# Moving the last pair's transposes of u from SyncE's DMA queue to ScalarE's, and its stores the other way

## The chip, the cores and the metric

The kernel runs on one core of a Trainium2 chip. The metric is the device time of one execution in microseconds. The core has five engines that run side by side and wait for each other through semaphores: TensorE (PE in the profile, with its weight loads apart as PEld), VectorE (DVE), ScalarE (ACT), GpSimd (POOL) and SyncE (SP). DMAs are issued by an engine's instruction stream, in its order: an issue that waits for its data also holds back the issues behind it. SPq and ACTq in the profile are the issues of SyncE and ScalarE.

## The reference

A chunked attention (chunks of 64 rows, 8 batches, 8 heads, 576 rows, head size 64) is followed by a mixing layer on rows of 512 numbers:

```python
attn = softmax(q_c @ k_c.T / sqrt(D)); x = attn @ v_c       # x: (8, 576, 512)
theta = x @ w_theta
zr, zi = x * cos(theta), x * sin(theta)
u = x + einsum('ts,bsd->btd', w_tok_r, zr) + einsum('ts,bsd->btd', w_tok_i, zi)
out = u + maximum(u @ w_ch, 0)
```

The change lies in the last line: u @ w_ch needs u turned (its rows as columns), and out has to be stored.

## The kernel before

The 8 batches are taken as 4 pairs, p = 0 to 3. The 2 x 576 rows of a pair make 9 tiles of 128 rows, j = 0 to 8; tile 4 (MID) holds the last 64 rows of both batches. Nothing is scheduled automatically: the string ORDER (lines 18 to 66) names every step, and each engine gets its share in that order. A step is a kind, a pair and tile, and for products a PSUM slot: `W.34.1` is the product u @ w_ch of pair 3, tile 4, in slot 1.

The steps at the end of a tile are these:

- `Y` (`y`, L480): nine products into ps_y (eighteen of half width for tile 4), the sum over rows of both einsums.
- `y` (`add_x`, L488): VectorE adds x and writes u in float16; there are seven buffers.
- `Ud` (`u_dma`, L505): one DMA transpose turns u (128 x 512) into uT; there are five buffers. The early tiles do this with TensorE instead (`U`, L497) and a copy.
- `W` (`w`, L517): four products of uT with w_ch into ps_uw.
- `w` (`relu_add`, L526): VectorE makes o = max(ps_uw, 0) + u in float32; there are four buffers.
- `st` and `sa` (`store`, L543): the 128 rows of o are two runs of 64 rows in the output, so a tile is stored by two DMAs of 128 KB, the lower half r = 0 and the upper half r = 1. In pairs 0 to 2 `st` stores both halves from SyncE. In pair 3 `st` stores the half r = 0 from SyncE, and `sa` the half r = 1 from ScalarE.

In the text below, "upper" is the half that `sa` stores (r = 1) and "lower" the half that `st` stores in pair 3 (r = 0).

In pair 3 all nine tiles are turned by DMA. The end of ORDER runs, in TensorE's view: Y.36, Y.34, W.35, W.33, W.37, W.36, W.34, and then ten products of zeros (`D`, L157) whose results nobody reads. The order of SyncE's issues in the same stretch: st.38, st.32, st.31, st.30, Ud.37, Ud.33, Ud.36, Ud.34, st.35, st.33, st.37, st.36, st.34. ScalarE issues sa.31, sa.38, sa.32, sa.30, sa.35, sa.33, sa.37, sa.36, sa.34. ScalarE's last computing step is the sine of pair 3, group D; behind it its stream has only these stores.

Each DMA of SyncE and ScalarE reports to one of eight semaphores, taken in turn, and waits for the one that used it before. A buffer of o or uT is written again only when its readers have ended.

Of the kernel before, what the change touches and what calls it, by code (L numbers as in the profile page):

```python
# [69 lines left out]
def kernel(  # L70
# [11 lines left out]
    nc = tc.nc  # L82
# [4 lines left out]
    NDB = DM // P  # L87
    NE = H // 2
    NP = B // 2
# [58 lines left out]
    st = {p: {} for p in range(NP)}  # L148
# [353 lines left out]
    def u_dma(p, j):  # L502
        uT = tmp.tile([P, DM], FP16, name="uT", bufs=5)
        st[p]["uT", j] = uT
        nc.sync.dma_start_transpose(uT.rearrange("p (a c) -> p a c", a=NDB), st[p]["u", j])  # L505

    def u_copy(p, j, copy):
        uT = tmp.tile([P, DM], FP16, name="uT", bufs=5)
# [14 lines left out]
    def relu_add(p, j):  # L523
# [3 lines left out]
            out=o, in0=st[p].pop(("ps_uw", j)), scalar=0.0, in1=u, op0=ALU.max, op1=ALU.add  # L527
        )
        st[p]["o", j] = o

    def store(p, j, queues):
        if j == MID:
            to = [out[2 * p + b, KT * P : S, :] for b in range(2)]
        else:
            bb = int(j > MID)
            jl = j - bb * (MID + 1)
            s0 = (jl // 2) * GT + (jl % 2) * CH
            to = [out[2 * p + bb, s0 + r * P : s0 + r * P + CH, :] for r in range(2)]  # L540
        for r, queue in enumerate(queues):
            if queue is not None:
                queue.dma_start(to[r], st[p]["o", j][half[r]])  # L543
# [45 lines left out]
        "y": add_x,  # L589
        "U": u_t,  # L590
        "Ud": u_dma,
        "ua": lambda p, j: u_copy(p, j, nc.scalar.copy),
        "uv": lambda p, j: u_copy(p, j, nc.vector.tensor_copy),
        "W": w,
        "w": relu_add,
        "st": lambda p, j: store(p, j, (nc.sync, nc.sync if p < 3 else None)),
        "sa": lambda p, j: store(p, j, (None, nc.scalar)),
    }
    with tc.manual_schedule():
        for step in ORDER:  # L600
# [33 lines left out]
```

The softmax here doesn't subtract the row's maximum and nothing guards it: scores larger than these inputs give would overflow.

## Time and profile before

The time is 203.63 us, the median of 3 runs (202.67 to 203.73). The profiled execution has a span of 201.2 us, at the full TensorE clock.

| engine or queue | busy | instructions |
|---|---|---|
| TensorE | 190.9 us (95%) | 2766 |
| VectorE | 127.8 us (63%) | 235 |
| ScalarE | 93.1 us (46%) | 100 |
| GpSimd | 106.3 us (53%) | 133 |
| stores from SyncE | 63 issues of 128 KB | landing after 2.9 us (median) |
| stores from ScalarE | 9 issues of 128 KB | landing after 2.7 us (median) |
| transposes uT<-u from SyncE | 22 issues | landing after 2.5 us (median) |

A busy share says little here, since the end of the kernel differs from its middle. In the last 10 us the engines work in a chain: TensorE makes ps_uw, VectorE o, and a queue stores it. What matters there is which step of that chain ends last for each tile, and what stands ahead of it in its queue. A line of the timeline names the start and the length in us, the engine, the line of the kernel and the tiles (out<-in); in square brackets is the engine's idle time before it and what ended that. Rows marked "x4" are four instructions in a row, and their length is that from the first's start to the last's end, waits between them included.

### The profile page before, as it was taken

What the parts mean: (1) busy time and instruction counts of PE and PEld (TensorE: products, weight loads), DVE (VectorE), ACT (ScalarE), POOL (GpSimd) and SP (SyncE); (2) the same over time, 40 slices, a digit from 0 to 9 for tenths busy, and PEclk for the clock granted to TensorE, in tenths of its full rate; (3) what the DMA queues carried; (4) which work ended last, traced back from release to release, by engine and by line L of the source; (5) the groups of instructions that cost most, each with busy time, mean ns of one, the idle gap of its engine ahead of it and who ended that gap; (6) DMA issues with size and microseconds to landing.
All of it is one profiled execution on the core that took longest, in us unless ns stands there. A gap on an engine that the chain in (4) does not pass through costs nothing.

```text
span 201.2 us, 6347 instructions
## 1 busy us (share of the span) xinstructions
PE 190.9 (95%) x2766; PEld 95.1 (47%) x2766; DVE 127.8 (63%) x235; ACT 93.1 (46%) x100; POOL 106.3 (53%) x133
## 2 busy tenths in 40 slices
PE   7988788999989999999999999999999799899986
PEld 2435455555544645455465555453444344344432
DVE  0015689387886867848874785977584566744461
ACT  2304967456922488797257976427800444000000
POOL 7999999798998999978998800000000000000000
DMA  5999999999999999999999992287777886573775
GB/s 190 173 169 155 159 186 166 153 173 145 168 187 187 155 171 205 181 216 158 161 207 157 153 223 64 45 142 108 159 122 145 174 169 148 121 159 62 214 163 171
DMA packets 140091, 32.01 MB, mean 159 GB/s; under 512 B 132769, under 2 KB 134945, under 8 KB 140065
## 3 DMA queue, kind: packets, MB, share of 16 engines
q0 software_dynamic: 114288, 16.02, 118.9%
q1 hardware_dynamic: 25056, 14.43, 31.2%
q10 hardware_dynamic: 720, 1.18, 2.0%
q8 instruction: 21, 0.34, 0.7%
q14 instruction: 6, 0.04, 0.1%
HBM read 33.06 MB, written 9.44 MB: 211 GB/s over the span
## 4 chain that ended last, share of the span: by engine, by line
PE 56%; DMA 22%; POOL 18%; issue 3%; DVE 0%; SPq 0%; POOLq 0%
PE ps_y L480 24%; PE ps_uw L517 12%; POOL qk L174 11%; PE ps_theta L410 10%; DMA v<-in_v_dram 7%; DMA uT<-u 6%; POOL v L182 4%; DMA qk<-in_q_dram 4%; DMA qk<-in_k_dram 3%; PE ps_qkT L262 2%; PE ps_x L341 2%; PE ps_sT L308 2%; DMA xT<-x 2%; POOL wnat L192 1%; PE ps_idle L157 1%
## 5 line engine op out<-in xcount | busy, mean ns | idle before, releaser
L480 PEld LDWEIGHTS <-wT 128*128 128x128 f16 (+1 forms) x360 | 30.8, 100 | 35.1 <-issue 1.4
L480 PE MATMUL ps_y<-zr,wT 128*128 128x512 f16 (+1 forms) x180 | 44.4, 381 | 0.0
L480 PE MATMUL ps_y<-zi,wT 128*128 128x512 f16 (+1 forms) x180 | 41.8, 379 | 0.0
L488 DVE TENSOR_TENSOR u<-ps_y,x 128x512 f16<-128x512 f32 x36 | 24.8, 688 | 25.0 <-PE ps_y L480 23.5
L517 PE MATMUL ps_uw<-wch,uT 128*128 128x512 f16 x144 | 36.4, 380 | 2.2 <-DMA uT<-u 2.2
L174 POOL DMA_DIRECT2D qk<-in_q_dram x40 | 34.1, 872 | 3.2 <-issue 1.0
L182 POOL DMA_DIRECT2D v<-in_v_dram x40 | 34.0, 869 | 2.9 <-issue 0.9
L174 POOL DMA_DIRECT2D qk<-in_k_dram x40 | 34.1, 869 | 2.3 <-issue 0.9
L410 PE MATMUL ps_theta<-wtheta,xT 128*128 128x512 f16 x144 | 34.3, 380 | 0.6 <-DMA xT<-x 0.5
L426 ACT ACTIVATE cos<-ps_theta,pihalf 128x1024 f16<-128x1024 f32 (+1 forms) x22 | 21.1, 961 | 26.2 <-PE ps_theta L410 23.2
L321 ACT ACTIVATE eT<-ps_sT 128x1024 f16<-128x1024 f32 (+1 forms) x20 | 18.6, 939 | 28.4 <-PE ps_sT L308 28.3
L526 DVE SCALAR_TENSOR_TENSOR o<-ps_uw,u 128x512 f32<-128x512 f32 x36 | 24.7, 689 | 10.9 <-PE ps_uw L517 10.6
L354 DVE TENSOR_TENSOR x<-ps_x,recip 128x512 f16<-128x512 f32 (+1 forms) x40 | 25.5, 638 | 1.4
L517 PEld LDWEIGHTS <-uT 128*128 128x128 f16 x144 | 12.8, 98 | 18.8 <-DMA uT<-u 4.8
L410 PEld LDWEIGHTS <-xT 128*128 128x128 f16 x144 | 13.2, 98 | 16.6 <-DMA xT<-x 0.9
L430 ACT ACTIVATE sin<-ps_theta 128x1024 f16<-128x1024 f32 (+1 forms) x22 | 19.0, 865 | 0.0
L157 PE MATMUL ps_idle<-blank 128*128 128x512 f16 x60 | 17.3, 435 | 1.3 <-DVE pihalf L145 1.2
L287 DVE COPY qkT<-ps_qkT 128x2048 f16<-128x2048 f16 x11 | 13.4, 1218 | 4.0 <-PE ps_qkT L262 4.0
L353 DVE RECIPROCAL recip<-ps_x 128x8 f32<-128x8 f32 (+1 forms) x40 | 7.9, 197 | 11.1 <-PE ps_x L341 10.9
L341 PE MATMUL ps_x<-v,eT 64*64 64x65 f16 x576 | 11.9, 196 | 2.2 <-DMA v<-in_v_dram 1.6
L262 PE MATMUL ps_qkT<-id,qk 64*128 64x64 f16 x576 | 12.0, 191 | 1.0 <-DMA qk<-in_k_dram 0.9
L341 PEld LDWEIGHTS <-eT 64*64 64x64 f16 x576 | 8.3, 106 | 9.4 <-issue 4.8
(42 smaller groups left out, 138.5 us busy)
## 6 DMA issues: line engine op xcount, KB each, us to landing
out_dram<-o SPq DMA_DIRECT2D x63, 128.0 KB, 2.9
qk<-in_q_dram POOLq DMA_DIRECT2D x32, 128.0 KB, 6.5
qk<-in_k_dram POOLq DMA_DIRECT2D x32, 128.0 KB, 6.4
v<-in_v_dram POOLq DMA_DIRECT2D x32, 128.0 KB, 6.5
out_dram<-o ACTq DMA_DIRECT2D x9, 128.0 KB, 2.7
theta<-in_moe_w_theta_dram SPq DMA_DIRECT2D x1, 1024.0 KB, 5.6
wnat<-in_moe_w_tok_r_dram POOLq DMA_DIRECT2D x2, 288.0 KB, 6.0
wnat<-in_moe_w_tok_i_dram POOLq DMA_DIRECT2D x2, 288.0 KB, 6.3
```

The costliest lines, as they stand in the source:

```text
L157: nc.tensor.matmul(ps, blank[:, 0:P], blank, start=True, stop=True)
L174: nc.gpsimd.dma_start(nats[p, g][rows, which, r], (q, k)[which][b, :, t0 : t0 + n, :].rearrange("h s d -> s h d"),)
L182: nc.gpsimd.dma_start(v16[rows, slot + r, :, 0:D], v[b, :, t0 : t0 + n, :].rearrange("h s d -> s h d"),)
L341: nc.tensor.matmul(psv[half[r], to, h4, :], eT[rows, h % 2, r if n == 2 else 0, h // 2, :], v16[rows, slot + (r if n == 2 else 0), h, 0 : ...
L354: nc.vector.tensor_tensor(out=st[p]["x"][:, j0 : j0 + n, f * NE * D : (f + 1) * NE * D].rearrange("p c (h d) -> p c h d", h=NE), in0=psv[: ...
L410: nc.tensor.matmul(ps[:, j * DM : j * DM + DM], xT[:, (j + (t or 0)) * NDB + db, :], wtheta16[:, db, :], start=(db == 0), stop=(db == NDB ...
L426: nc.scalar.activation(out=cos[:, 0:n].rearrange("p a e -> p (a e)"), in_=pin, func=AF.Sin, bias=pihalf, scale=1.0,)
L430: nc.scalar.activation(out=sin[:, 0:n].rearrange("p a e -> p (a e)"), in_=pin, func=AF.Sin)
L480: nc.tensor.matmul(ps[rows], wT[:, kt, cols], z[:, jz, :], start=(kt == 0), stop=(kt == 2 * KT),)
L488: nc.vector.tensor_tensor(out=u, in0=st[p].pop(("ps_y", j))[:, 0:DM], in1=st[p]["x"][:, j], op=ALU.add)
L517: nc.tensor.matmul(ps, uT[:, db * P : db * P + P], wch16[:, db, :], start=(db == 0), stop=(db == NDB - 1),)
L526: nc.vector.scalar_tensor_tensor(out=o, in0=st[p].pop(("ps_uw", j)), scalar=0.0, in1=u, op0=ALU.max, op1=ALU.add)
```

## The change

The nine transposes of pair 3 are issued from ScalarE, and the nine stores of `sa` from SyncE, so that in pair 3 both halves of every tile leave from SyncE's queue. ORDER stays as it is. The purpose is that a transpose does not stand behind stores which wait for o: ScalarE's stream holds only transposes then.

```diff
     def u_dma(p, j):
         uT = tmp.tile([P, DM], FP16, name="uT", bufs=5)
         st[p]["uT", j] = uT
-        nc.sync.dma_start_transpose(uT.rearrange("p (a c) -> p a c", a=NDB), st[p]["u", j])
+        queue = nc.scalar if p == NP - 1 else nc.sync
+        queue.dma_start_transpose(uT.rearrange("p (a c) -> p a c", a=NDB), st[p]["u", j])
...
         "st": lambda p, j: store(p, j, (nc.sync, nc.sync if p < 3 else None)),
-        "sa": lambda p, j: store(p, j, (None, nc.scalar)),
+        "sa": lambda p, j: store(p, j, (None, nc.sync)),
```

SyncE's stream at the end then reads: st.38, sa.38, st.32, st.31, sa.32, sa.30, st.30, sa.35, sa.33, st.35, st.33, and both halves of 37, 36 and 34. ScalarE's: Ud.31, Ud.32, Ud.38, Ud.30, Ud.35, Ud.37, Ud.33, Ud.36, Ud.34.

## The prediction

> **What bounds the kernel now.** I read the chain of waits first, for its last pieces, then the same stretch engine by engine, and last the queues. Only the last pair of batches (p = 3) is touched, so only the time after about 172 us matters. The chain there is TensorE work with three short gaps. Below: start and length in us, and what held the chain.
>
> ```profile
> 171.82 1.04 PE ps_uw L517 x4
> ...
> 189.80 2.44 DMA uT<-u
> 192.24 0.18 DVE o L526
> 192.42 3.18 DMA uT<-u
> 195.65 1.04 PE ps_uw L517 x4
> ```
>
> TensorE itself, in the timeline (in brackets its idle time, and what ended it):
>
> ```profile
> 191.15 1.04 PE L517 MATMUL ps_uw<-wch,uT 128*128 128x512 f16 x4
> 192.35 2.84 PE L517 MATMUL ps_uw<-wch,uT 128*128 128x512 f16 x12 [0.17 <-DMA uT<-u]
> 195.65 1.04 PE L517 MATMUL ps_uw<-wch,uT 128*128 128x512 f16 x4 [0.45 <-DMA uT<-u]
> ```
>
> These are W.35, then W.33, W.37 and W.36, then W.34. The table by stretch has TensorE busy 13.70 of 13.70 us from 177.5 to 191.2, so earlier u transposes of p = 3 held nobody up; only the last five products wait. SyncE's queue shows why:
>
> ```profile
> 185.08 3.27 SPq L543 DMA_DIRECT2D out_dram<-o x4
> 188.45 5.19 SPq L505 DMA_TRANSPOSE uT<-u x4
> 193.74 4.17 SPq L543 DMA_DIRECT2D out_dram<-o x5
> ```
>
> The four transposes of tiles 37, 33, 36 and 34 go out one behind the other, after stores that themselves wait for o. u of tile 37 was ready at 181.3, and its transpose left at 188.45. After the last o (DVE, 196.72 to 197.41) the two stores of tile 34 leave at the same moment from two queues, and this ends the kernel. For these two:
>
> ```profile
> L543 SPq DMA_DIRECT2D out_dram<-o x1: 466/466/466, 197.4 to 197.4; - x1
> L543 ACTq DMA_DIRECT2D out_dram<-o x1: 498/498/498, 197.4 to 197.4; - x1
> ...
> DMA to landing us min/median/max: 2.4/2.5/2.7
> ```
>
> So from the last issue (197.44) to the end of the span (201.25) it is 3.8 us: up to 2.7 to land, some 1.1 to close the program.
>
> **What the skill says.** The Trainium skill, "DMA: Bandwidth & Descriptors", section "Issuing engines are not separate DMA queues": issuing from several engines saves only the issuing sequencer's time, usually small beside the transfer. The trace agrees on the size (0.5 to 0.6 us of issue against 2.4 to land), but here some ten issues stand in a row at the end, so that this saving is what counts. Same page, "Silent corruption: two transposing streams in flight at once": the first transpose of a second issuing engine must wait until those of the first have landed. The built program carries this wait on ScalarE's first transpose (Ud.31); the trace before has one stream only and can't show its cost. Same page, "Anatomy of one DMA": about 2 us per DMA are fixed; its fit for GpSimd's queue gives 2.0 + 131072/436000 = 2.3 us for a store, and the trace has 2.4 to 2.7 for stores from SyncE and ScalarE.
>
> **Transposes to ScalarE: what is won.** ScalarE has nothing after its last sine (167.64, 1.02 us), so each transpose leaves when its u is ready or, if that is later, 1.25 us after the one before it. With u ready as now (end of each add on DVE): Ud.31 waits for Ud.20, issued at 171.86 and 2.42 us on its way, to 174.28; with about four more semaphore waits of some 0.06 us it leaves at 174.5 and lands at about 176.95, where W.31 wants it at 177.53. Ud.32 lands at 178.2 (W.32 at 182.35), Ud.38, 30 and 35 before 185.8, Ud.37 at about 187.0, Ud.33 (u at 186.99) at 189.5, Ud.36 (u at 189.88) at 192.4, Ud.34 (u at 191.95) at 194.45. W.33 can now follow W.35 at 192.03 rather than 192.35, W.36 ends near 194.65, and W.34 starts there instead of 195.65. TensorE ends 1.0 us earlier: 0.17 + 0.45 us of idle time, and twice the 0.18 us by which four products last longer (1.04) than their pitch (0.86) when the pipeline is empty. This is all that the transposes can give, for before 191.2 TensorE is full.
>
> **Stores to SyncE: what is lost.** Until 189.4 SyncE keeps up: tiles 31, 38, 32 and 30 are stored there in pieces while DVE makes the next o. From w.35 on, ten stores stand in SyncE's queue, in the order 35 upper, 33 upper, 35 lower, 33 lower, then 37, 36 and 34 in pairs. Before, they lay five on each queue. The price of one comes from a stretch where nothing waited for data:
>
> ```profile
> 158.01 2.46 SPq L543 DMA_DIRECT2D out_dram<-o x4
> 160.52 1.35 SPq L393 DMA_TRANSPOSE xT<-x  x1
> ```
>
> Four stores and the gaps are 160.52 - 158.01 = 2.51 us, and a wait of its own for o before the first adds some 0.06 a pair: 0.63 to 0.65 us a store. The two ends: 0.47 us (a store that had just waited, as in the two lines above) and 0.82 us (3.27/4, which includes a wait for o). I take 0.63, since most of these find their o ready.
>
> w.35 ends at 192.91 as now. W.33 from 192.03 gives w.33 from 193.10 (1.07 us later, as w.35 follows W.35) to 193.79, so 33 upper leaves at 193.83. Eight stores are behind it; the last starts at 193.83 + 8 x 0.63 = 198.87. VectorE is no longer the limit: o of 37 and 36 are ready at about 194.7 and 195.5, while SyncE reaches them at 195.7 and 197.0. There is one new wait: o of tile 34 takes the buffer of tile 35 (four o buffers), whose lower half now leaves at 194.36 and lands at 196.8. So w.34 runs 196.8 to 197.5 and not from 195.75; but SyncE gets to its stores at 198.25, and this is hidden.
>
> **Sum.** The last store leaves at 198.87 instead of 197.44: + 1.43 us. It lands alone, some 2.4 us later, not as one of two halves issued together of which the slower took 2.7: - 0.3 us. The closing is the same. + 1.1 to + 1.15 us on the span; on the median 203.63 this gives 204.8 us.
>
> **Rivals.** *The store pitch is shorter and the gain pays for most of it.* At 0.55 us a store, the last starts at 193.83 + 4.4 = 198.23, + 0.8 - 0.3 = + 0.5 us: 204.1 us, no change that can be told. For it: the first store after a wait takes 0.47. Against: every unhindered row of stores in the trace has about 0.63.
>
> *ScalarE's transposes become a wait of TensorE.* Ud.31 has only 0.6 us to spare before W.31, and one transpose in this trace (issued 167.15) took 4.6 us to land. If Ud.31 does the same, it lands at 179.1, TensorE stands still for 1.6 us, and everything behind shifts: 203.63 + 1.6 + 1.1 = 206.3 us. For it: the full drain of the other stream. Against: the three transposes after the slow one landed in 2.4 us each.
>
> *Faster: SyncE keeps up.* Then the end is set by w.34. If only TensorE's end counted, w.34 would end at 196.43 and the two stores leave one after the other, the second at 196.95: - 0.5 - 0.3 = - 0.8 us, 202.8 us. For it: TensorE is the bound of the whole kernel, and 1.0 us of its waits does go. Against: with four o buffers w.34 must wait for the lower half of tile 35 to land, and even at 0.47 us a store this is 194.3 + 2.4, so that w.34 ends at 197.4, as now. It takes an issue of about 0.35 us, which no row shows, or luck in an earlier wait, such as that slow transpose which costs TensorE 0.54 us at 171.3.
>
> **How the numbers follow.** Main forecast (+ 0.8 to + 1.6 us) 0.64; shorter pitch 0.22; TensorE waits 0.07; faster 0.07. The line at + 0.5% is 1.02 us, close to the middle of the main case; I put 0.50 of its 0.64 above it, since creeping landings (a row of four lands 2.3, 2.4, 2.4, 2.5 us after issue) and a w.33 that is not earlier (+ 0.3) both lengthen it. Slower: 0.50 + 0.07 = 0.57; same: 0.14 + 0.22 - 0.02 = 0.34; faster: 0.09, with 0.02 from the shorter pitch for the 0.5 us by which runs of the kernel before differ (202.67 to 203.73). The range, from the short pitch at 204.1 less that scatter to the long end of the main case (+ 1.6 and the same scatter), is 203.5 to 205.8.
>
> **What would show it.** Right: no gap of TensorE between W.35 and W.34, W.34 at about 194.7; ten stores back to back on SyncE to about 199.4, the last starting 1.4 us later than now; an idle VectorE before the last o that ends with a store's landing; Ud.31 leaving when Ud.20 has landed. Wrong: SyncE idle between the last stores, a store pitch of 0.5 or 0.8 us, TensorE waiting before W.31, or transposes on ScalarE that take longer than 1.25 us to issue or 2.4 to land.

## The result, and the profile after

The changed kernel takes 204.69 us (median of 20 runs) beside 203.60 us for the kernel before (20 runs): + 1.09 us. The ratio is 1.0067, with a 95% interval of 1.0041 to 1.0093; the forecast was + 1.1 to + 1.15 us and 204.8 us. Here and below the medians are of all runs, and the ratios with their intervals of those within 1.5% of the fastest run of the same kernel, so a ratio need not be the quotient of two medians.

The profiled execution after has a span of 202.9 us, 1.7 us longer than the one before. Of that, 0.7 us was there before the end part begins: w.35, the first of the last five steps on VectorE, ends at 193.61 instead of 192.91. That point lies between 191.8 and 194.2 in the fourteen profiles of this study, and two profiles of one and the same kernel (the one with the late halves and Ud.20 moved, below) have it at 192.68 and 191.82. So I count from it; whether a part of the 0.7 us comes from the change is not shown. From the end of w.35 to the end of the span it was 8.33 us before and is 9.31 after: + 0.98 us.

TensorE after, from W.35 to W.34 in the timeline:

```profile
191.84 4.65 PE L518 MATMUL ps_uw<-wch,uT 128*128 128x512 f16 x20
196.33 1.24 PE L157 MATMUL ps_idle<-blank 128*128 128x512 f16 x3
198.25 1.89 PE L157 MATMUL ps_idle<-blank 128*128 128x512 f16 x8 [0.68 <-DVE o L527]
```

The five products are now one row of twenty matmuls in 4.65 us. Before, they took from 191.15 to 196.69, 5.54 us, in three pieces with a wait for uT between them. The transposes have given 0.89 us. The new gap of 0.68 us stands behind the last product, among the products of zeros.

ScalarE's queue (its last sine, then nothing but transposes) and SyncE's:

```profile
168.48 1.02 ACT L430 ACTIVATE sin<-ps_theta 128x1024 f16<-128x1024 f32 x1
175.53 18.35 ACTq L506 DMA_TRANSPOSE uT<-u  x9
```

```profile
185.77 14.33 SPq L543 DMA_DIRECT2D out_dram<-o  x17
```

SyncE's last store ends its issue at 200.1, where both queues were done at 197.9 before. The ten stores behind w.35, by the tile o:

```profile
L543 SPq DMA_DIRECT2D out_dram<-o x10: 467/568/604, 193.6 to 199.5; - x10
...
DMA to landing us min/median/max: 2.2/2.4/2.4
```

The first row gives the shortest, median and longest issue in ns and when the first and last began. From the end of w.35 to the start of the last issue it is 5.9 us. Before, it was 4.5 us, to a pair that left together from two queues.

VectorE, with the step w of tiles 35, 33, 37, 36 and 34:

```profile
192.92 0.69 DVE L527 SCALAR_TENSOR_TENSOR o<-ps_uw,u 128x512 f32<-128x512 f32 x1 [0.27 <-PE ps_uw L518]
193.78 0.69 DVE L527 SCALAR_TENSOR_TENSOR o<-ps_uw,u 128x512 f32<-128x512 f32 x1 [0.17 <-PE ps_uw L518]
194.72 0.69 DVE L527 SCALAR_TENSOR_TENSOR o<-ps_uw,u 128x512 f32<-128x512 f32 x1 [0.25 <-PE ps_uw L518]
195.59 0.69 DVE L527 SCALAR_TENSOR_TENSOR o<-ps_uw,u 128x512 f32<-128x512 f32 x1 [0.17 <-PE ps_uw L518]
197.51 0.69 DVE L527 SCALAR_TENSOR_TENSOR o<-ps_uw,u 128x512 f32<-128x512 f32 x1 [1.23 <-DMA out_dram<-o]
```

Of the same steps before, the first two:

```profile
192.22 0.69 DVE L526 SCALAR_TENSOR_TENSOR o<-ps_uw,u 128x512 f32<-128x512 f32 x1 [0.27 <-DMA uT<-u]
193.43 0.69 DVE L526 SCALAR_TENSOR_TENSOR o<-ps_uw,u 128x512 f32<-128x512 f32 x1 [0.51 <-PE ps_uw L517]
```

After, the first four follow TensorE's products, and w.33 comes 0.86 us behind w.35 instead of 1.21. The last waits 1.23 us for a store to land, the lower half of tile 35, whose buffer it takes. This wait is the most visible line of the profile after, and it costs nothing, as the run with a spare buffer shows.

### The profile page after: what moved, and what is told of

Read it like the earlier page. It is cut to its first block, busy times and chain, and to the rows that moved or that the text cites. A ratio compares the mean times of both kernels' runs of the same rounds, so it can differ in the third digit from the quotient of the medians.

```text
span 202.9 us, 6342 instructions
## 1 busy us (share of the span) xinstructions
PE 191.1 (94%) x2766; PEld 95.4 (47%) x2766; DVE 127.5 (63%) x235; ACT 93.1 (46%) x100; POOL 106.2 (52%) x133
## 4 chain that ended last, share of the span: by engine, by line
PE 59%; POOL 18%; DMA 18%; issue 3%; DVE 1%; SPq 0%; DVEq 0%; POOLq 0%
PE ps_y L480 26%; PE ps_uw L518 13%; POOL qk L174 11%; PE ps_theta L410 11%; DMA v<-in_v_dram 7%; POOL v L182 5%; DMA qk<-in_q_dram 4%; DMA wch<-in_moe_w_ch_dram 3%; PE ps_qkT L262 2%; PE ps_x L341 2%; PE ps_sT L308 2%; DMA xT<-x 2%; POOL wnat L192 1%; DMA uT<-u 1%; DMA out_dram<-o 1%
## 5 line engine op out<-in xcount | busy, mean ns | idle before, releaser
L410 PE MATMUL ps_theta<-wtheta,xT 128*128 128x512 f16 x144 | 35.1, 386 | 1.1 <-DVE xT L384 0.4
L157 PE MATMUL ps_idle<-blank 128*128 128x512 f16 x60 | 16.8, 422 | 2.0 <-DVE pihalf L145 1.2
```

Source lines behind the costliest of these rows:

```text
L410: nc.tensor.matmul(ps[:, j * DM : j * DM + DM], xT[:, (j + (t or 0)) * NDB + db, :], wtheta16[:, db, :], start=(db == 0), stop=(db == NDB ...
```

## The experiments

The expectations name the theories. A: what stands in an in-order queue sets the end, here ten stores in SyncE's. B: the bytes to be stored set it (in the two half changes and the last versions, the rival is stated in the text). C: the last o waits too long for its buffer.

**A spare buffer for the last o.**

```diff
-        o = outp.tile([P, DM], FP32, name="o32")
+        if p == NP - 1 and j == MID:
+            o = nat.tile([P, 2 * DM], FP32, name="qk16")[:, 0:DM]
+        else:
+            o = outp.tile([P, DM], FP32, name="o32")
```

> The changed kernel, but o of tile 34 has a buffer of its own (one of the dead q and k buffers), so it waits for no store. A: the last o is ready about 1.7 us earlier, and SyncE still gets to it at the same time: 204.7 us, no change against the changed kernel. C: the end moves with the last o, 1 us or more earlier: 203.6 us or less. B: 204.7 us.

Measured: 204.50 us beside 203.45, ratio 1.0054 (1.0030 to 1.0078). VectorE's last step and the last two stores:

```profile
196.51 0.69 DVE L530 SCALAR_TENSOR_TENSOR qk<-ps_uw,u 128x512 f32<-128x512 f32 x1 [0.25 <-PE ps_uw L518]
```

```profile
193.62 5.18 SPq L546 DMA_DIRECT2D out_dram<-o  x8
198.90 1.18 SPq L546 DMA_DIRECT2D out_dram<-qk  x2
```

The last o is ready at 197.21, and its stores leave at 198.90 and 199.48: 5.89 us from w.35 to the last store, as in the changed kernel. C falls. An o that waits 1.2 us for a landing, and a store that then waits 1.7 us in the queue, are the same end.

**Half the bytes, as many stores.** 

```diff
-                queue.dma_start(to[r], st[p]["o", j][half[r]])
+                n = DM // 2 if p == NP - 1 else DM
+                queue.dma_start(to[r][:, 0:n], st[p]["o", j][half[r]][:, 0:n])
```

> The changed kernel with as many stores, but in pair 3 each stores only 256 of the 512 columns (the other half of the output of pair 3 is left out). A (the number of issues in SyncE's queue sets the end): the same pitch, the last store leaves as in the changed kernel and lands perhaps 0.2 us sooner: 204.5 us. Rival B (bytes): half of the time of the row of stores goes, 3 us less at most, down to where the last o ends: 203 us.

Measured: 204.21 us beside 203.26, ratio 1.0035 (1.0013 to 1.0058).

```profile
L544 SPq DMA_DIRECT2D out_dram<-o x10: 466/564/596, 193.4 to 199.2; - x10
...
DMA to landing us min/median/max: 1.9/2.0/2.1
```

The issues take what they took with all the bytes (466/564/596 against 467/568/604 ns), and from w.35 to the last store it is 5.87 us. Half the bytes only land 0.3 to 0.4 us sooner. B falls for the row of stores; bytes count at the landing of the last one.

**Whole tiles by one store.** In `store`, for pair 3 and all tiles but tile 4:

```diff
+        if p == NP - 1 and j != MID:
+            if queues[0] is not None:
+                bb = int(j > MID)
+                jl = j - bb * (MID + 1)
+                nc.sync.dma_start(out[2 * p + bb, jl * P : jl * P + P, :], st[p]["o", j])
+            return
```

> The changed kernel, but in pair 3 each tile but tile 4 is stored by one DMA of 256 KB from SyncE to 128 rows that follow each other (the rows of pair 3 stand in another order in the output). Bytes and buffers are as in the changed kernel, the issues behind w.35 are six instead of ten. A: SyncE keeps up with VectorE, the two stores of tile 34 leave one after the other when its o is ready, the second about 0.6 us after it: 203.2 us. B: 204.7 us. C: 203.2 us.

Measured: 203.15 us beside 203.45, ratio 0.9979 (0.9955 to 1.0003).

```profile
192.94 3.02 SPq L538 DMA_DIRECT2D out_dram<-o  x4
196.55 1.13 SPq L549 DMA_DIRECT2D out_dram<-o  x2
```

SyncE now waits for every o instead of being waited for. From w.35 to the last store it is 4.18 us and to the end of the span 7.58 us, with the same bytes as in the changed kernel. The issues are fewer, six instead of ten, and four of them are shorter as well (0.33 us, see the last section); this run does not part the two. Together with the run before, it shows A: what SyncE spends on issuing, not what the stores carry.

**The late upper halves on ScalarE.** Behind Ud.34 ScalarE has nothing left to turn, so its stores can hold up no transpose. Of ORDER, only the part that differs is shown, its lines joined.

```diff
-w.35 sa.35 Ud.33 W.33.0 w.33 sa.33 W.37.1 Ud.36 Ud.34 w.37
+w.35 Ud.33 W.33.0 w.33 W.37.1 Ud.36 Ud.34 sa.35 sa.33 w.37
...
-        "sa": lambda p, j: store(p, j, (None, nc.sync)),
+        "sa": lambda p, j: store(p, j, (None, nc.scalar if j in (5, 3, 7, 6, 4) else nc.sync)),
```

> The changed kernel, but the upper halves of tiles 35, 33, 37, 36 and 34 are stored from ScalarE, behind its last transpose. Theory A (ten stores in one queue set the end): the ten stores are five and five again and the transposes stay early, so W.34 starts about 3.5 us after W.35 and the last pair of stores leaves as soon as the last o is there: 1.0 us less than before, 202.6 us. Rival B (the end is set by the bytes that the DMA engines have to move after W.35): the same bytes, so 204.7 us as in the changed kernel. Rival C (the last o waits for a buffer that is stored too late): 35's lower half leaves at once here, so C too gives less, about 202.6; the run with a spare buffer tells C from A.

Measured: 203.01 us beside 203.45, ratio 0.9991 (0.9964 to 1.0018). All of the loss is gone, and of the gain that A said (202.6 us) the times show nothing; the end part shows 0.6 us of it. The stores by the tile o:

```profile
L543 SPq DMA_DIRECT2D out_dram<-o x5: 466/467/469, 194.2 to 197.9; - x5
L543 ACTq DMA_DIRECT2D out_dram<-o x5: 498/527/557, 194.5 to 197.9; - x5
...
DMA to landing us min/median/max: 2.3/2.8/3.0
```

From w.35 to the last store it is 3.70 us, 0.83 less than before; but the last pair takes 2.8 and 3.0 us to land, where it was 2.4 and 2.7. Pairs now leave 0.9 to 1.0 us apart up to the last, which before left 1.5 us behind the one ahead of it; that this is the reason is not shown. Up to the end of the span it is 7.75 us, 0.58 less than before.

**The upper halves on GpSimd.**

```diff
-        "sa": lambda p, j: store(p, j, (None, nc.sync)),
+        "sa": lambda p, j: store(p, j, (None, nc.gpsimd)),
```

> The changed kernel, but the upper halves of pair 3 are stored from GpSimd, which is idle there. A: any second queue will do; an issue there took 0.87 us for the loads of this kernel, as much as a product takes, so it just keeps up, and the last leaves with the last o: 202.8 us if a store from GpSimd lands as fast as one from SyncE, up to 203.8 us if its issue and landing take a microsecond more. B: 204.7 us.

Measured: 204.08 us beside 203.45, ratio 1.0004 (0.9972 to 1.0036), 8.25 us from w.35 to the end of the span. GpSimd's issues:

```profile
196.14 0.53 POOL L543 DMA_DIRECT2D out_dram<-o  x1 [0.34 <-DVE o L527]
197.23 0.53 POOL L543 DMA_DIRECT2D out_dram<-o  x1 [0.56 <-DVE o L527]
```

They take 0.53 us, not the 0.87 of the loads, so this queue keeps up too; each begins 0.27 us after SyncE's for the same o, and the last lands 2.55 us later. From the last landing (199.78) to the end of the span (201.4) it is 1.6 us, where the other kernels have 1.0 to 1.1. Why was not tried. The median is above the 202.8 to 203.8 us that A gave and 0.6 us above the kernel before, while the ratio shows no difference, and its interval lies just below that of the changed kernel (from 1.0041). So the loss goes with this queue too, less surely than with ScalarE's, and nothing is gained beyond that.

**Each half of the change alone.** First only the transposes on ScalarE (`sa` stays `nc.scalar`), then only the stores on SyncE (`u_dma` stays `nc.sync`); ORDER is that of the kernel before.

> Only the first half of the change: the nine transposes of pair 3 are issued from ScalarE, and the upper halves are still stored from there. In ScalarE's queue the stores of 35 and 33 then stand ahead of Ud.33 and Ud.36. Theory A (a queue is in order, and what stands behind a store waits for that store's o): Ud.33 leaves only after w.35, W.33 waits some 3.9 us for it, Ud.36 and Ud.34 leave only after w.33, and W.34 starts about 6.3 us later than in the kernel before: 210 us. Rival B (the transposes do not gain from their order, only from being on another engine): W.34 early as in the changed kernel, 202.6 us, since stores are again on two queues.

> Only the second half of the change: both halves are stored from SyncE, and the transposes stay there. A: the same blocked transposes as with the first half alone (35 upper ahead of Ud.33, 33 upper ahead of Ud.36), and behind Ud.34 eight stores at 0.63 us in one row: 211 us. Rival B (the stores' queue costs 1.4 us at the end and nothing else): 205.1 us.

Measured: 213.53 us beside 203.26 for the first, ratio 1.0482 (1.0418 to 1.0546); 210.82 us for the second, ratio 1.0386 (1.0316 to 1.0455), with four runs each. SyncE's queue in the second:

```profile
192.24 0.47 SPq L543 DMA_DIRECT2D out_dram<-o  x1
192.80 1.24 SPq L505 DMA_TRANSPOSE uT<-u  x1
197.99 0.47 SPq L543 DMA_DIRECT2D out_dram<-o  x1
198.55 2.56 SPq L505 DMA_TRANSPOSE uT<-u  x2
201.16 5.06 SPq L543 DMA_DIRECT2D out_dram<-o  x8
```

Store, transpose, store, transposes: the order of ORDER, and each transpose leaves as soon as the store ahead of it has its o. The eight stores of the last row have 0.64 us each. A said 211 and got 210.8, in part by luck: TensorE had half its clock for a while (last section), so that the four matmuls of W.33, ahead of all this, took 1.89 us (from 195.34) instead of 1.04. A had not counted that. The first half alone shows the same pattern in ScalarE's queue, and TensorE behind it:

```profile
196.85 3.17 PE L518 MATMUL ps_uw<-wch,uT 128*128 128x512 f16 x8 [4.35 <-DMA uT<-u]
202.69 1.04 PE L518 MATMUL ps_uw<-wch,uT 128*128 128x512 f16 x4 [2.67 <-DMA uT<-u]
204.21 1.89 PE L518 MATMUL ps_uw<-wch,uT 128*128 128x512 f16 x4 [0.48 <-DMA uT<-u]
```

The waits stand where A put them (4.35 where 3.9 was said), but W.34 starts 8.6 us later than before (204.21, 195.65), not 6.3, and the time is over the expected 210 by 2.3 us in the profiled execution and by 3.5 in the median. TensorE's slower clock made W.33 and W.34 longer by 0.42 and 0.85 us, and the last three transposes took 2.9 to 3.0 us to land, where the prediction counts 2.4. Neither half is worth anything by itself: with this ORDER each needs the other to have a queue without a store ahead of a transpose.

**The late halves with Ud.20 moved.** In all kernels so far with transposes on ScalarE, TensorE waited 0.15 to 0.5 us for Ud.20 or Ud.22, which stand in SyncE's queue behind stores. Ud.20 can leave sooner (again only the part of ORDER that differs):

```diff
-st.28 y.20 H.3C.0 g.3B z.3B W.23.1 g.3D w.23 Y.31.0 Y.32.1 y.31 W.22.0 st.23 g.3C Ud.20 z.3C
+st.28 y.20 Ud.20 H.3C.0 g.3B z.3B W.23.1 g.3D w.23 Y.31.0 Y.32.1 y.31 W.22.0 st.23 g.3C z.3C
```

> As the run with the five late upper halves on ScalarE, but Ud.20 stands ahead of the stores of tile 23 in SyncE's queue, right behind the step that makes its u. That transpose was held up there by stores that wait for o, and TensorE waited 0.2 to 0.5 us for it near 175 us in every run so far with the transposes on ScalarE. A: this wait goes, and with it the wait of Ud.31 for Ud.20: 0.3 us less than with the late halves alone, 202.7 us. Rival (an earlier transpose only moves the wait to the next product): 203.0 us.

> The kernel before, with nothing but Ud.20 moved ahead of the stores of tile 23 in SyncE's queue. It tells whose the gain of the last version is. Theory A (the late halves on ScalarE give 0.6 us by themselves at the end, and the moved transpose 0.2 to 0.5 us near 175 us): 0.3 us less than before, and the time from the end of w.35 to the end of the span stays at about 8.3 us. Rival (the moved transpose is the whole gain): 0.6 us less than before or more. In the trace of the kernel before, TensorE waited there for Ud.22, not for Ud.20; if that is the usual case without transposes on ScalarE, there is no gain at all.

Measured: 202.60 us beside 203.26 for the late halves with this, ratio 0.9972 (0.9950 to 0.9994); 202.92 us beside 203.58 for the kernel before with this alone, ratio 0.9970 (0.9946 to 0.9993). That would make the moved transpose the whole gain, as the rival said, while the end parts of the two profiles differ by 0.55 us (7.73 against 8.28 from w.35 to the end), as A said. Both were therefore run again on one chip, with a third that also has the spare buffer.

> The same kernel as the one with the late halves on ScalarE and Ud.20 moved, again, beside the kernel before with Ud.20 moved, on one chip. Theory A (the end part gives 0.6 us of its own, 7.73 instead of 8.3 us from the end of w.35): 0.6 us less than that one, ratio to the kernel before 0.994. Rival (the whole gain is the moved transpose): the same ratio as that one, 0.997.

> The kernel before with Ud.20 moved, again, on the chip of the one with the late halves. A and rival alike: ratio 0.997; it is the measure for the other.

> As the first of these three, and o of tile 34 has a buffer of its own, so that w.34 does not wait for the upper half of 35 to land (it started 1.0 us after w.36 there, where a product takes 0.9). A: 0.1 us less than the first, ratio 0.9935, with about 7.65 us from the end of w.35 to the end. Rival: 0.997 like the others.

Measured beside 203.12 us: 201.99 us, ratio 0.9942 (0.9919 to 0.9965); 203.10 us, ratio 0.9998 (0.9975 to 1.0020); with the spare buffer 202.91 us (14 runs), ratio 0.9990 (0.9955 to 1.0024). From w.35 to the end of the span: 7.72, 8.34 and 7.66 us. On one chip the late halves are worth 1.1 us by the medians, against nothing in the pair of runs before. The end part, which the profiles give to 0.1 us, says 0.6 us both times. What the moved transpose is worth stays open between nothing and 0.6 us, and the spare buffer's 0.1 us is below what these runs can tell. The version with the late halves and Ud.20 moved was faster than the kernel before in both of its runs, by 0.3% and 0.6%. But the one with the spare buffer, which should have been faster still (0.9935 was said, and its interval leaves that out), shows no gain, although its end part is the shortest of all. What happens ahead of w.35 differs by more than what is sought here, so a gain of this size is not secured.

## Why the prediction was right

*The stores' pitch.* Said: 0.63 us, last store at 5.96 us after w.35 (198.87 - 192.91). Measured: the eight stores from 33 upper (194.50) to the last (199.50) have 5.00/8 = 0.625 us, the last leaves 5.89 us after w.35. The half-bytes run shows that this is a price of the issue, as the prediction took it. The Trainium skill ("DMA: Bandwidth & Descriptors", "Issuing engines are not separate DMA queues") calls the saved sequencer time usually small beside the transfer. One issue is (0.6 against 2.4 us), but here it was multiplied: 5.89 - 4.53 = 1.36 us.

*The landing.* Said: 2.4 us instead of 2.7. Measured: 2.37 instead of 2.70 (200.145 - 197.44 before). The closing is 1.04 us, where the prediction kept the 1.10 of before.

*The transposes.* Said: 1.0 us earlier. Measured: 0.89. The missing 0.1 us is in the pitch of the products. By the PSUM slots in ORDER (1, 0, 1, 0, 1), TensorE needs w.35 done before it can fill the same PSUM slot with W.37, and w.33 before W.36, so that every second of VectorE's steps follows at 0.94 instead of 0.86 us (192.92, 193.78, 194.72, 195.59). The prediction had this at 0.86 throughout. The slots as the reason are argued, not tried; the 0.1 us is hidden behind the stores.

*The first transpose's wait.* Said: Ud.31 leaves some 0.2 us after Ud.20 has landed, and W.31 does not notice. Measured: Ud.20 lands at 175.36, Ud.31 leaves at 175.53 and lands at 178.03; TensorE has no gap before W.31. It had one of 0.39 us just before, for Ud.20 itself. The Trainium skill ("DMA: Bandwidth & Descriptors", "Silent corruption: two transposing streams in flight at once") asks for the full completion, and the trace shows it as 0.17 us of issue after a landing. The rival that saw TensorE waiting for it did not come.

*The transposes' landing.* Said: 2.4 us. Measured, for the nine: 2.4 to 3.9, median 3.2. Five that lay beside a row of SyncE's stores took 3.2 to 3.9, the other four 2.4 to 2.6; whether the stores are the cause was not tried. Here the prediction was off by 0.8 us in the middle and 1.5 at worst, and one of its own signs of being wrong appeared (three of the issues too, up to 1.42 us, are over its 1.25). Nothing came of it: TensorE waited for none of the nine.

*The new wait of the last o.* Said: w.34 starts 3.9 us after the end of w.35, hidden. Measured: 197.51 - 193.61 = 3.9, and hidden (spare buffer: no change).

*The sum.* + 1.36 for the last issue, - 0.33 for the landing, - 0.06 for the closing: + 0.97, where the end parts differ by 0.98. Against that the forecast was some 0.15 us high, 0.07 of it in the last issue and the rest in the landing and the closing. That it comes closer still to the medians' + 1.09 is luck: the interval of the ratio leaves 0.8 to 1.9 us open.

Of the 0.89 us gained on TensorE, 0.35 us counted, as the prediction had it: w.33 follows w.35 sooner, and the row of stores without a gap begins with the upper half of 33. The rest bought nothing, because the stores, not the last product, ended the kernel.

## What to carry to other kernels

In the last microseconds count the issues in each queue: with one product every 0.9 us, two stores of 0.63 us per tile no longer fit into one queue, and what TensorE gains after their row has begun is lost. In an in-order queue a transfer that others wait for must not stand behind one that itself waits for data; but once its last such transfer has left, the queue is free for stores again, which is how the late upper halves take the loss of this change away. And a long wait that ends with a DMA's landing, seen beside a full queue, may cost nothing: give it its own buffer and see.

## What the runs showed of the hardware

A store of 128 rows (256 KB) took 332 ns to issue, one of 64 rows (128 KB) some 470 to 490 ns after a wait and 540 to 600 ns behind another:

```profile
L538 SPq DMA_DIRECT2D out_dram<-o x4: 332/332/333, 192.9 to 195.6; - x4
L549 SPq DMA_DIRECT2D out_dram<-o x2: 492/538/584, 196.6 to 197.1; - x2
```

The larger one also landed no later, 2.0 to 2.3 us after its issue. Whether the number of rows or the one contiguous target of those stores makes the difference was not tried.

In both half changes TensorE ran at half its clock for a while. In the one with the transposes alone on ScalarE, by stretches that end where the granted clock changes (the columns of interest are TensorE's busy time, behind the comma, and, behind POOL, the granted clock):

```profile
193.91:197.32 3.41, 0.47 (x3) 0.24 (x4) 0.00 (x0) 0.00 (x0) 0.00 (x0) 1.00 0.48 115
197.32:200.73 3.41, 2.70 (x7) 0.69 (x5) 1.36 (x2) 0.00 (x0) 0.00 (x0) 0.50 0.16 32
200.73:204.15 3.42, 1.04 (x4) 0.31 (x4) 0.41 (x2) 0.00 (x0) 0.00 (x0) 1.00 0.81 176
204.15:207.56 3.41, 3.24 (x7) 0.95 (x8) 0.99 (x2) 0.00 (x0) 0.00 (x0) 0.50 0.40 99
```

In two stretches of 3.41 us the granted clock was 0.50, behind stretches of the same length in which TensorE had worked for 0.47 and 1.04 us. The matmuls of 128 x 512 took 0.62 us (median of the sixteen behind W.35) instead of 0.38. In the kernel with the stores alone on SyncE there are two such stretches as well, behind 0.00 and 1.07 us of work. The Trainium skill ("TensorE: Matmul & The Clock Gate", "Part 1: The HAM clock gate (the "warmup" mystery)") has half the clock after an idle window of about 3.4 us. The 0.50 agrees; but the second stretch of each kernel came behind a window in which TensorE had worked for about 1 us, and in the one shown behind an idle time of 2.67 us. A long wait is thus paid twice, and the expectations for both runs, which counted the wait alone, left this out.
